# Batch 0's v on GpSimd's DMA queue ahead of w_in, q's halves from two queues, no f32 weight columns, j 8 later

## The chip, the cores and the metric

The kernel runs on one core of one Trainium2 chip. The metric is the device time of one execution in microseconds (us), given as the median of several executions. A profile shows one execution. Its span, from the first to the last instruction, is about 1.8 us shorter than the device time of the same execution (287.6 against 289.42 us for the kernel before).

## The reference

Eight batches of linear attention feed a two-layer block with a sine activation. Shapes: q, k, v are 8 x 8 heads x 576 tokens x 64; w_in is 512 x 2048, w_out 2048 x 512, alpha 2048; all f32.

```
q_s = softmax(q, over the 64 features)       # without 1/sqrt(d)
k_s = softmax(k, over the 576 tokens)
kv  = einsum('bhsd,bhse->bhde', k_s, v)
x   = einsum('bhsd,bhde->bhse', q_s, kv)      -> 4608 tokens x 512
h   = x @ w_in
g   = h + sin(alpha * h)**2 / (alpha + 1e-9)
out = g @ w_out
```

## The kernel before

The 4608 tokens are handled in nine tiles of 512. A tile takes 64 matmuls for h and 64 for the output, so TensorE is the engine to keep busy. One batch has 576 tokens, cut into nine slices of 64 ("j 0 to 8"; slice j holds the tokens 9p + j). Tile 0 needs only batch 0 (512 of its tokens, j 0 to 7), and tile 1 needs the other 64 tokens of batch 0 (j 8) and 448 of batch 1. Each engine works through its instructions in the order written below.

The start, as far as the change touches it:

```python
nc.scalar.dma_start(out=alpha_rows, in_=moe_alpha...)       # 8 KB, ScalarE's queue
load("q", q, 0, halves=True)                                # two transfers, sync queue
load("k", k, 0, halves=True)                                # two transfers, sync queue
for ii, j0, j1 in ((0, 0, 9), (1, 0, 5), (1, 5, 9)):
    nc.sync.dma_start(out=st[:, ii::2, j0:j1]..., in_=src_view(v, 0)...)
for x in range(2):                                          # w_in columns 0:256, as f32
    nc.sync.dma_start(out=wf[64 * x:64 * x + 64], in_=win_v[x][:, :, 0:256])
# ... identity, zeros ...
nc.tensor.transpose(tpa, alpha_rows, ident[0:nN, 0:nN])
DVE_CP(alpha_sb, tpa)                    # VectorE, ahead of everything on q
nc.vector.reciprocal(inva_sb, alpha_sb)
exp_q(0); exp_k(0)                       # ScalarE, one activation for each half
warm_up(7)
norm_q(0, [V, V])                        # VectorE: reduce, reciprocal, multiply; twice
GP_CP(held, staged["k", 0][:, 0, 0, 0:1])                   # GpSimd waits for k
for c0, c1 in ((256, 512), (512, 1024), (1024, 1536)):
    load_win(c0, c1)                     # GpSimd's queue, cast to bf16 in flight
GP_CP(win[:, :, 0:256], wf)              # the f32 columns, cast on GpSimd
load_win(1536, 2048); load_wout(0); load_wout(1)
# ... transposes of q, casts of v, two kv products, kv_norm -> kbd,
#     four attention products, copied to xT by ScalarE and VectorE in turn;
#     then the matmuls of h for tile 0 ...
```

Between tile 0 and tile 1 the 64 output matmuls of tile 0 are dealt out one by one (`take`) among the attention of batch 1:

```python
take(os, 10); [j 8 products of batch 0]; ACT_CP(xT[...], xp); take(os, 36)
exp_q(1); load("v", v, 1, halves=True); load_batch(2)
norm_q(1, ...); exp_k(1); q_transpose(1, ...); cast_v(1, [ACT_CP, DVE_CP])
take(os, 8)
kv_mm(1, 0); kv_norm(1, 0, 1); take(os, 2)
kv_mm(1, 1); kv_norm(1, 1, 2); take(os, 1)
# two pairs of attention products, each followed by take(os, 2); then take(os): the last 3
# then h of tile 1
```

The softmax here doesn't subtract the row's maximum and nothing guards it: scores larger than these inputs give would overflow.

## Time and profile before

The kernel took 289.31 us (median of 4, 289.01 to 289.61). These moments from the timeline:

| moment | us from the start |
|---|---|
| q's halves land / alpha lands | 4.50 and 5.98 / 2.83 |
| VectorE's first reduce of q starts | 5.72 |
| v's three pieces land | 10.96, 11.85, 12.97 |
| second kbd done / f32 columns of w_in cast | 14.92 / 16.17 |
| first h matmul of tile 0 | 16.23 |
| first output matmul of tile 0 | 30.05 |
| v of batch 1 lands (two halves) | 41.33, 42.71 |
| first h matmul of tile 1 | 47.76 |

### The profile page before, as it was taken

The numbers are of one execution on the slowest core, as the hardware profiler recorded it, in microseconds if no ns is written. First come the engines' busy times: TensorE is split into PE (matmuls) and PEld (weight loads), VectorE is DVE, ScalarE is ACT, GpSimd is POOL, SyncE is SP. The second block draws the span as 40 slices with busy tenths as digits, with TensorE's granted clock in tenths as the row PEclk, the third lists the DMA queues.
The fourth block names the chain that finished last, engine by engine and source line by source line (L and its number), as shares of the span: only waits on it lengthen the run. The fifth ranks groups of instructions, "written<-read, shape, count | busy, mean of one in ns | idle before, by whom it ended". The sixth has DMA issues, their size and how long they took to land.

```text
span 287.6 us, 4234 instructions
## 1 busy us (share of the span) xinstructions
PE 273.7 (95%) x1542; PEld 130.8 (45%) x1570; DVE 188.6 (66%) x280; ACT 227.2 (79%) x321; POOL 79.8 (28%) x73
## 2 busy tenths in 40 slices
PE   2889999999999999999999999999999999999994
PEld 1434454445454445444544454445444444444443
DVE  3867595889958667856776677757674555555412
ACT  5799775999479999899889988998877777777500
POOL 0679420675775571005300440032000000000000
PEclk9999999999999999999999999999999999999998
DMA  7999999935899957129910990116011111111142
GB/s 257 341 205 245 267 401 407 309 150 161 196 153 404 392 187 128 38 43 368 275 32 22 331 333 8 38 39 136 19 39 36 36 36 39 36 38 36 46 103 73
DMA packets 37893, 46.03 MB, mean 160 GB/s; under 512 B 15968, under 2 KB 21360, under 8 KB 37872
## 3 DMA queue, kind: packets, MB, share of 16 engines
q1 hardware_dynamic: 33392, 41.69, 47.5%
q0 software_dynamic: 4288, 3.93, 8.4%
q8 instruction: 12, 0.20, 0.3%
q10 hardware_dynamic: 192, 0.14, 0.2%
q14 instruction: 9, 0.07, 0.1%
HBM read 36.71 MB, written 9.44 MB: 160 GB/s over the span
## 4 chain that ended last, share of the span: by engine, by line
PE 83%; DMA 5%; POOL 4%; DVE 3%; issue 2%; SPq 1%; ACT 1%; POOLq 0%
PE hp L234 36%; PE op L254 34%; PE hp L254 4%; DMA st_w<-in_moe_w_in_dram 3%; POOL s L244 3%; PE kvp L157 2%; PE xp L206 2%; PE hh L234 1%; DMA qT<-qn 1%; PE op L538 1%; PE op L234 1%; ACT s L240 1%; DVE g L250 1%; DVE qs L144 1%; SPq L94 1%
## 5 line engine op out<-in xcount | busy, mean ns | idle before, releaser
L250 DVE SCALAR_TENSOR_TENSOR g<-s,inva_sb,hp 128x512 bf16<-128x512 f32 x130 | 96.2, 746 | 64.2 <-ACT s L242 54.2
L234 PE MATMUL hp<-xT,win 128*128 128x512 bf16 x512 | 129.2, 379 | 1.2 <-POOL win L320 0.6
L254 PE MATMUL op<-wout,g 128*128 128x512 bf16 x479 | 121.9, 379 | 1.1 <-issue 0.5
L240 ACT ACTIVATE s<-hp,alpha_sb 128x512 f32<-128x512 f32 x130 | 87.7, 682 | 25.8 <-PE hp L234 25.0
L234 PEld LDWEIGHTS <-win 128*128 128x128 bf16 x576 | 56.1, 98 | 68.3 <-POOL win L320 1.1
L254 PEld LDWEIGHTS <-g 128*128 128x128 bf16 x560 | 54.1, 98 | 61.7 <-issue 0.8
L242 ACT ACTIVATE s<-s 128x512 f32<-128x512 f32 x112 | 70.5, 630 | 3.5
L146 POOL TENSOR_TENSOR qn<-qe,qs 128x1152 bf16<-128x1152 bf16 x12 | 25.3, 2126 | 74.3 <-DVE qs L140 63.1
L244 POOL TENSOR_TENSOR s<-s 128x512 f32<-128x512 f32 x29 | 30.5, 1062 | 22.2 <-ACT s L240 21.6
L260 DVE COPY o<-op 128x512 f32<-128x512 f32 (+2 forms) x33 | 22.1, 670 | 9.7 <-PE op L254 5.8
L117 ACT ACTIVATE ke<-st_k 128x1152 bf16<-128x1152 f32 x16 | 17.9, 1151 | 3.0 <-DMA st_k<-in_k_dram 3.0
L117 ACT ACTIVATE qe<-st_q 128x1152 bf16<-128x1152 f32 x16 | 17.8, 1155 | 2.4 <-DMA st_q<-in_q_dram 2.3
L139 DVE TENSOR_REDUCE qs<-qe 128x36 f32<-128x2304 bf16 x5 | 12.8, 2553 | 8.7 <-ACT qe L117 8.6
L131 POOL CAST vb<-st_v 128x1152 bf16<-128x1152 f32 x12 | 13.6, 1162 | 10.1 <-DMA st_v<-in_v_dram 10.1
L254 PE MATMUL hp<-wout,g 128*128 128x512 bf16 x62 | 14.8, 379 | 0.2 <-issue 0.2
L209 DVE CAST xT<-xp 128x512 bf16<-128x512 f32 (+1 forms) x18 | 13.4, 743 | 0.0
L144 DVE TENSOR_REDUCE qs<-qe 128x18 f32<-128x1152 bf16 x6 | 8.0, 1330 | 4.6 <-ACT qe L117 4.6
L157 PE MATMUL kvp<-vb,ke 64*128 64x130 bf16 x288 | 9.9, 217 | 0.3 <-ACT vb L310 0.3
L117 ACT ACT_TABLE_LOAD x7 | 9.0, 1283 | 1.3 <-PEq L552 1.2
L157 PEld LDWEIGHTS <-ke 64*128 64x128 bf16 x288 | 8.2, 93 | 3.9 <-ACT s L242 1.3
L234 PE MATMUL hh<-xT,win 128*128 128x512 bf16 x39 | 9.4, 379 | 0.1
L206 PE MATMUL xp<-qT,kbd 128*128 128x256 bf16 (+1 forms) x40 | 8.2, 286 | 0.4 <-DVE xT L209 0.3
(68 smaller groups left out, 117.3 us busy)
## 6 DMA issues: line engine op xcount, KB each, us to landing
out_dram<-o SPq DMA_DIRECT2D x70, 128.0 KB, 2.4
st_q<-in_q_dram SPq DMA_DIRECT2D x6, 1152.0 KB, 6.6
st_k<-in_k_dram SPq DMA_DIRECT2D x6, 1152.0 KB, 8.5
st_v<-in_v_dram SPq DMA_DIRECT2D x6, 1152.0 KB, 10.3
st_q<-in_q_dram SPq DMA_DIRECT2D x4, 576.0 KB, 5.1
st_k<-in_k_dram SPq DMA_DIRECT2D x4, 576.0 KB, 7.1
wout<-in_moe_w_out_dram POOLq DMA_DIRECT2D x4, 512.0 KB, 9.6
st_v<-in_v_dram SPq DMA_DIRECT2D x3, 576.0 KB, 9.2
```

Source lines behind the costliest of these rows:

```text
L117: nc.scalar.activation(dst[:, :, ii * 128:(ii + 1) * 128].rearrange("p j (x d) -> p x j d", x=2), src[:, ii::2], AX.Exp)
L131: engs[ii](vv[:, 2 * ii:2 * ii + 2, :, 0:D], staged["v", b][:, ii::2])
L146: engs[ii % len(engs)].tensor_tensor(qn[:, ii].rearrange("p j (x d) -> p j x d", x=2), qe[:, ii], part.unsqueeze(3).to_broadcast([128, J, ...
L157: nc.tensor.matmul(kvp[:, e, ii * 130:(ii + 1) * 130], ke[r, j, ii * 128:(ii + 1) * 128], vt[r, j, ii * 130:(ii + 1) * 130], start=(j == 0 ...
L206: nc.tensor.matmul(xp[:, e, 0:n], kt[:, e, ii], qT[:, ii, j0:j1, e * 64:(e + 1) * 64], start=True, stop=True)
L234: nc.tensor.matmul(hp, win[:, ki, ni * 128:(ni + 1) * 128], xT[:, ki, t * MF:(t + 1) * MF], start=(ki == 0), stop=(ki == 3))
L240: nc.scalar.activation(s, hp, AX.Sin, scale=alpha_sb[:, ni:ni + 1])
L242: nc.scalar.activation(s, s, AX.Square)
L244: nc.gpsimd.tensor_tensor(s, s, s, op=ALU.mult)
L250: nc.vector.scalar_tensor_tensor(G[t][:, ni], in0=s, scalar=inva_sb[:, ni:ni + 1], in1=hp, op0=ALU.mult, op1=ALU.add)
L254: nc.tensor.matmul(acc, G[t][:, ni, j * 128:(j + 1) * 128], wout[:, ni, :], start=(ni == 0), stop=(ni == nN - 1))
L260: eng(o[:, cols], acc)
```

## The change

The intent is to feed the first h matmul sooner. GpSimd's f32 cast of the first 256 columns of w_in, which ended the wait for that matmul, goes away; v is requested on GpSimd's queue, followed at once by all of w_in; q's two halves are requested at the same moment from two queues; and the j 8 products move behind ten more output matmuls, with their copy on VectorE.

```diff
+    for ii, eng in ((0, nc.sync), (1, nc.scalar)):
+        eng.dma_start(out=st...[:, ii::2], in_=src_view(q, 0)[:, ii::2])
     nc.scalar.dma_start(out=alpha_rows, in_=moe_alpha...)
-    load("q", q, 0, halves=True)
     load("k", k, 0, halves=True)
-    [v in three pieces on nc.sync]
-    [w_in columns 0:256 as f32 on nc.sync]
 ...
+    GP_CP(held, staged["q", 0][:, 0, 0, 0:1])          # GpSimd waits for q's first half
+    [v in the same three pieces on nc.gpsimd]
+    for c0, c1 in ((0, 256), (256, 512), (512, 1024), (1024, 1536), (1536, 2048)):
+        load_win(c0, c1)
+    load_wout(0); load_wout(1)
 ...
-    [held on k; load_win of 256 to 1536; GP_CP(win[:, :, 0:256], wf); load_win(1536, 2048); w_out]
 ...
-        take(os, 10)
+        take(os, 20)
         [j 8 products]
-        ACT_CP(xT[:, :, 8 * P:9 * P], xp)
-        take(os, 36)
+        DVE_CP(xT[:, :, 8 * P:9 * P], xp)
+        take(os, 26)
```

More of the change, by code (lines that the diff above doesn't have):

```diff
@@ L268 @@
     V, GP = nc.vector, nc.gpsimd
+    staged["q", 0] = st = stage.tile([128, 4, J, D], F32, name="st_q", tag="st")
+    for ii, eng in ((0, nc.sync), (1, nc.scalar)):
+        eng.dma_start(out=st.rearrange("p i j d -> p i (j d)")[:, ii::2], in_=src_view(q, 0)[:, ii::2])
     nc.scalar.dma_start(out=alpha_rows, in_=moe_alpha.rearrange("(no ni) -> no ni", ni=128))
-    load("q", q, 0, halves=True)
     load("k", k, 0, halves=True)
-    staged["v", 0] = st = stage.tile([128, 4, J, D], F32, name="st_v", tag="st")
-    VJ = ((0, 0, 9), (1, 0, 5), (1, 5, 9))
-    for ii, j0, j1 in VJ:
-        nc.sync.dma_start(out=st[:, ii::2, j0:j1].rearrange("p i j d -> p i (j d)"),
-                          in_=src_view(v, 0)[:, ii::2, j0 * D:j1 * D])
-    wf = stage.tile([128, 4, J, D], F32, name="st_w", tag="st")[:, :, 0:4].rearrange("p c a b -> p c (a b)")
-    for x in range(2):
-        nc.sync.dma_start(out=wf[64 * x:64 * x + 64], in_=win_v[x][:, :, 0:256])
     make_identity(nc, ident)
@@ L298 @@
     nc.vector.reciprocal(inva_sb, alpha_sb)
+    GP_CP(singles.tile([128, 1], F32, name="held"), staged["q", 0][:, 0, 0, 0:1])
+    staged["v", 0] = st = stage.tile([128, 4, J, D], F32, name="st_v", tag="st")
+    for ii, j0, j1 in ((0, 0, 9), (1, 0, 5), (1, 5, 9)):
+        GP.dma_start(out=st[:, ii::2, j0:j1].rearrange("p i j d -> p i (j d)"),
+                     in_=src_view(v, 0)[:, ii::2, j0 * D:j1 * D])
+    for c0, c1 in ((0, 256), (256, 512), (512, 1024), (1024, 1536), (1536, 2048)):
+        load_win(c0, c1)
+    for c in range(2):
+        load_wout(c)
     exp_q(0)
@@ L315 @@
     q_tile(0)
-    GP_CP(singles.tile([128, 1], F32, name="held"), staged["k", 0][:, 0, 0, 0:1])
-    for c0, c1 in ((256, 512), (512, 1024), (1024, 1536)):
-        load_win(c0, c1)
-    GP_CP(win[:, :, 0:256], wf)
-    load_win(1536, 2048)
-    for c in range(2):
-        load_wout(c)
     q_transpose_ii(0, 0, 0, 8, tps[0])
```

## The prediction

> **What bounds the kernel now.** I read the table of cores first: one core, 287.6 us, granted clock 0.997, so nothing is throttled. Then the page: TensorE is busy 95% of the span, and its idle time is nearly all in the first slices. The table of stretches says how much: in 16.2 to 30 us the matmuls fill 13.66 of 13.80 us, and in 100 to 140 us 39.63 of 40.
>
> ```profile
> PE 273.7 (95%) x1542; PEld 130.8 (45%) x1570; DVE 188.6 (66%) x280; ACT 227.2 (79%) x321; POOL 79.8 (28%) x73
> 0.00:16.20 16.20, 8.86 (x72) 4.33 (x72) 10.94 (x24) 10.54 (x13) 6.48 (x15) 1.00 0.97 288
> 16.20:30.00 13.80, 13.66 (x62) 6.27 (x65) 9.55 (x16) 13.05 (x21) 12.08 (x14) 1.00 1.21 242
> 30.00:33.00 3.00, 2.72 (x17) 1.19 (x15) 2.58 (x6) 1.29 (x3) 2.29 (x3) 1.00 1.21 231
> ```
>
> After the stretch and its length come the busy times of TensorE, weight loads, VectorE, ScalarE and GpSimd, then clock, DMA share and GB/s. A busy TensorE need not be at its rate, so I checked the rate: in the chain of waits 16 matmuls of h take 3.45 us, 0.2157 each. The 64 of the first token tile at that rate are 13.80 us; the first starts at 16.23 and the output matmuls start at 30.05, which is 13.82 later. So from 16.23 on TensorE has work without a hole, and **the change can save what it brings that start forward, plus holes of a few tenths later**.
>
> What holds the start? In the timeline of the first microseconds (start, length, what, and in brackets the idle time before it and what ended it):
>
> ```profile
> 4.53 1.16 ACT L117 ACTIVATE qe<-st_q 128x1152 bf16<-128x1152 f32 x1 [2.02 <-DMA st_q<-in_q_dram]
> 5.72 1.35 DVE L144 TENSOR_REDUCE qs<-qe 128x18 f32<-128x1152 bf16 x1 [2.00 <-ACT qe L117]
> 10.37 1.36 DVE L146 TENSOR_TENSOR qn<-qe,qs 128x1152 bf16<-128x1152 bf16 x1
> 13.00 0.63 ACT L310 CAST vb<-st_v 128x512 bf16<-128x512 f32 x1 [0.81 <-DMA st_v<-in_v_dram]
> 14.33 0.59 DVE L170 TENSOR_TENSOR kbd<-kvp,kvr 64x128 bf16<-64x128 f32 x2
> 14.96 1.36 DVE L342 CAST xT<-hp 128x512 bf16<-128x512 f32 x2
> 15.13 1.04 POOL L320 CAST win<-st_w 128x1024 bf16<-128x1024 f32 x1 [2.32 <-DMA st_w<-in_moe_w_in_dram]
> 16.23 1.90 PE L234 MATMUL hp<-xT,win 128*128 128x512 bf16 x7 [0.65 <-POOL win L320]
> ```
>
> Two paths end together. The weights: the f32 columns land at 15.00 and GpSimd's cast ends at 16.17. The attention: the first xT piece is done at 15.34 (half of ScalarE's pair from 14.69), the last at 16.32 (VectorE's pair from 14.96). The chain names the weights, 9.68 us of DMA. With the weights free, the first matmul could go at 15.34, but the sixth (row ni=0, ki=3) would still wait for 16.32.
>
> **What the Trainium skill says.** *DMA: Bandwidth & Descriptors*, "Issuing engines are not separate DMA queues": DMAs from sync, scalar and gpsimd share the same 16 engines, and several issuers save only issue time. The trace agrees: in 2 to 12 us the engines are full (281 to 407 GB/s), so a second issuer adds no bandwidth there.
>
> The same page, "Queues, rings and completion order", has each engine go round the rings packet by packet. The trace looks more like first come, first served. Batch 1's q is requested at 24.60 while w_out is under way, and for two microseconds only GpSimd's queue moves:
>
> ```profile
> DMA packets 414, 0.41 MB, mean 205 GB/s; under 512 B 13, under 2 KB 414, under 8 KB 414
> q0 software_dynamic: 414, 0.41, 123.6%
> ```
>
> That is 24.6 to 26.6 us. Likewise w_in, requested from 8.75, has 8 packets through by 13.0. So v, requested on GpSimd's queue while k is under way, should neither overtake k nor wait for long.
>
> *SBUF — State Buffer*, the box on the "DVE blocks DMA" trap: VectorE in a two-port mode locks GpSimd out of writing descriptors. Here, six w_in requests beside a busy VectorE took 0.62 to 0.84 us each; if the lock acts, it costs some 0.2 us. *TensorE: Matmul & The Clock Gate*, Part 1: the array runs at half clock until it has been busy some 3.4 us. The trace agrees: seven warm-up matmuls from 5.74 take 3.15 us (0.45 each), the six from 9.65 take 1.49 (0.25).
>
> **The change part by part.**
>
> *Weights.* Gone are two f32 transfers (0.5 MB), their two requests and the 1.04 us cast. The first 256 columns come cast in flight, right behind v. Single transfer records show v landing at 10.96, 11.85 and 12.97, but most engines are through with v near 11.5 and one or two lag by 1.5 us. The column packets took 60 ns each against 46 for the f32 ones, so 256 columns take about 1.5 us: from 11.5, with the laggards, they should land between 13.2 and 14.5. That is 1.7 to 3 us before 16.17. The weights leave the path. GpSimd has eight semaphores for its DMAs, so its ninth request waits for the first v; enough is queued by then.
>
> *q from two queues, alpha behind it.* Before, the q halves land at 4.50 and 5.98 and alpha at 2.83. Now both halves are requested at about 0.74 and share the engines. By sharing evenly, both land near 5.3 to 5.7 (the bytes are those that landed by 5.98, less a faster ramp: the first full half microsecond is 3.0 to 3.5). So the first exponential, due at 4.53, starts near 5.4. And alpha is now behind the second half in ScalarE's ring, so it lands near 5.5. This matters, because the order of instructions keeps alpha's copy and reciprocal on VectorE ahead of the first reduce: before, from landing (2.83) to the end of that reciprocal (3.72) was 0.9 us, so VectorE can't begin to reduce before about 6.4. Either way the reduce moves from 5.72 to about 6.6: a delay **d of 0.9 us**. If the rings are served in turn by whole requests, q's first half lands as before and alpha alone sets d, 0.3 to 0.7.
>
> *What d does.* From 5.72 to 12.6 VectorE has no gap, and TensorE's transposes and first kv product hang on it, so the first kbd ends at 13.98 + d. The second product was bound by v's last piece (0.26 us of wait), so some of d vanishes. With d = 0.9: kbd ends at 14.88, reciprocal 0.18 and second kbd 0.59 with short gaps end at 15.72, two xT copies of 0.68 on VectorE end at 17.12. The sixth matmul of h starts there, and 59 x 0.2157 = 12.73 follow: 29.85 against 30.05, a gain of 0.2. By the same sum d = 0.3 (last copy 16.52) gains 0.8, d = 0 gains 1.0, d = 1.5 loses 0.4. Break-even is d = 1.1.
>
> *j 8 later.* Ten more output matmuls go ahead of the small attention products. Before, those waited for a buffer:
>
> ```profile
> 32.74 0.28 PE L214 MATMUL xp<-qT,kbd 128*128 128x64 bf16 x4 [0.28 <-DVE g L250]
> 33.06 0.37 ACT L396 CAST xT<-xp 128x256 bf16<-128x256 f32 x1 [1.74 <-PE xp L214]
> 33.45 1.28 ACT L117 ACT_TABLE_LOAD   x1
> ```
>
> Ten matmuls (2.16 us) cover the wait until the buffer comes free: a gain of 0.28. The copy moves to VectorE, which idles 2.59 us before its next reduce; ScalarE can load the exponential's table up to 1.7 us sooner. But batch 1's k and v are set by DMA (38.28 and 41.35), and TensorE has output matmuls in that time, so this is hidden.
>
> *Transfers sooner.* The first 25 us move the same source bytes, without the slack around 12 to 14 us where the rate was half. Weights, w_out and batch 1 should land about 1 us earlier. From 33 to 48 us TensorE idles only 0.21 more, mostly in normalisation steps that no DMA sets; from 70 to 100 us it idles 0.86. I put 0.15 on all of this.
>
> **The rivals.** (1) *The intended result*: neither split nor alpha costs anything and v's tail comes sooner; start gain 1.0, sum 1.4, 288.1 us. For it: the weights are what the chain names. Against: alpha's place in the ring. (2) *A new wait takes over*: q's first half and alpha late, so VectorE's chain replaces the weights; start gain 0.2, sum 0.6, 288.9. I think this the likeliest. (3) *v late or in k's way*: GpSimd is held until q's first half lands, then a 0.71 us copy and three requests of 0.6 to 0.8, the last near 8.4 if q lands at 5.4; k is done at 9.47, so there is some margin, but if the rings shared fairly, k would land later, exponentials of k and ScalarE's copies behind it would slide by 1 us or more, and the start would be 0.5 us later than before: 289.8. Against it: the first-come behaviour above. (4) *The transfer hidden anyway*: TensorE bound by ScalarE or VectorE just after the start, so that an earlier start buys only waiting. Against: in 16.2 to 30 us TensorE, not they, has no holes; it would make 289.3.
>
> **Range and chances.** Start: 0.55 x 0.2 + 0.3 x 0.8 - 0.15 x 0.4 = 0.29. With 0.28 for the buffer wait and 0.15 for the transfers: 0.72 us, from 289.55 to 288.8. The three runs of before spread over 0.6 us. The rivals span 288.1 to 289.8; with the spread I take 287.8 to 289.7. A change of 2% is 5.8 us; TensorE's whole idle time after 16.2 us is under 7 us, more than half of it at the very end, so faster by 2% gets 0.01, and slower, which would need a stalled queue, 0.01.
>
> **What would show it.** Right: no GpSimd cast of w_in; the first h matmul waits for xT, not for a DMA; first h between 15.3 and 16.2, first output matmul at 29.1 to 30.0; alpha lands after 5 us; the first reduce starts at 6.2 to 6.9; no VectorE wait before the j 8 products. Wrong in size: the first reduce still near 5.7 (then rival 1), or k's landing beyond 9.8 (rival 3). Wrong in kind: a wait of h for w_in columns, or holes in TensorE between 17 and 30 us.

## The result

The changed kernel took 289.62 us (median of 4, 289.56 to 289.95), where the kernel before took 289.31. The ratio is 1.0013 with a 95% interval of 0.9996 to 1.0030: the same. The 0.7 us that were expected did not come.

First the page of the changed kernel (its line on busy times), then its table of stretches, with the columns as in the prediction:

```profile
PE 275.4 (96%) x1570; PEld 130.8 (45%) x1570; DVE 188.6 (66%) x281; ACT 226.5 (79%) x320; POOL 81.7 (28%) x77
0.00:16.20 16.20, 8.18 (x70) 4.08 (x70) 9.41 (x22) 9.43 (x11) 10.24 (x21) 1.00 0.96 265
16.20:30.00 13.80, 13.65 (x63) 6.14 (x64) 10.19 (x18) 13.22 (x22) 9.47 (x11) 1.00 1.21 233
30.00:33.00 3.00, 2.98 (x14) 1.27 (x13) 2.48 (x6) 2.92 (x4) 2.92 (x3) 1.00 1.18 266
```

TensorE's total rose by 1.7 us although it does the same work: 1570 matmul records were kept against 1542. So this line can't be compared to a microsecond. The stretch of 30 to 33 us can: TensorE has no hole there now.

The timeline of the changed kernel shows the start. The columns are as in the prediction: start, length, engine and line, what, and in brackets the idle time before it.

```profile
5.80 2.22 ACT L117 ACTIVATE qe<-st_q 128x1152 bf16<-128x1152 f32 x2 [2.71 <-DMA st_q<-in_q_dram]
6.58 0.25 PE L289 MATMUL warm<-ident,alpha_rows 16*128 16x16 f32 x1 [6.58 <-DMA alpha_rows<-in_moe_alpha_dram]
6.87 0.17 DVE L290 COPY alpha_sb<-warm 128x16 f32<-128x16 f32 x1 [4.43 <-PE warm L289]
7.25 1.29 DVE L144 TENSOR_REDUCE qs<-qe 128x18 f32<-128x1152 bf16 x1
15.70 0.59 DVE L170 TENSOR_TENSOR kbd<-kvp,kvr 64x128 bf16<-64x128 f32 x2
16.35 0.60 PE L214 MATMUL hp<-qT,kbd 128*128 128x512 bf16 x2 [0.24 <-DVE kbd L170]
16.79 1.52 PE L234 MATMUL hp<-xT,win 128*128 128x512 bf16 x6
```

VectorE stands idle for 4.43 us and then does alpha before it does q, because that is the order of its instructions. Its first reduce starts at 7.25 instead of 5.72, and everything behind it slides: the second kbd ends at 16.29 instead of 14.92, and the first h matmul is at 16.79, 0.56 us later than before. The weights are no longer what it waits for: the first columns land at 13.08 and 13.73.

The chain of waits (start, length, what) of the changed kernel names the same two things in its first 50 us:

```profile
1.27 5.18 DMA alpha_rows<-in_moe_alpha_dram
...
33.27 10.52 DMA st_v<-in_v_dram
```

The second line is v of **batch 1**. It lands at 42.35 and 43.79, 1.0 and 1.1 us later than before, and tile 1's h starts at 48.26, 0.50 us later. The experiments need both lines.

### The profile page after: what moved, and what is told of

It reads as the page before. It is cut to its first block, busy times and chain, and to the rows that moved or that the text cites. A ratio compares the mean times of both kernels' runs of the same rounds, so it can differ in the third digit from the quotient of the medians.

```text
span 287.8 us, 4258 instructions
## 1 busy us (share of the span) xinstructions
PE 275.4 (96%) x1570; PEld 130.8 (45%) x1570; DVE 188.6 (66%) x281; ACT 226.5 (79%) x320; POOL 81.7 (28%) x77
## 4 chain that ended last, share of the span: by engine, by line
PE 76%; DMA 7%; DVE 6%; ACT 4%; POOL 3%; issue 2%; ACTq 0%; SPq 0%; POOLq 0%
PE hp L234 34%; PE op L254 33%; DMA st_v<-in_v_dram 4%; POOL s L244 3%; ACT s L240 3%; PE kvp L157 2%; DMA alpha_rows<-in_moe_alpha_dram 2%; DVE qs L144 2%; PE xp L206 2%; DMA qT<-qn 1%; PE op L534 1%; PE op L234 1%; PE hh L234 1%; DVE qn L146 1%; DVE o L260 1%
## 5 line engine op out<-in xcount | busy, mean ns | idle before, releaser
L254 PE MATMUL op<-wout,g 128*128 128x512 bf16 x496 | 124.2, 379 | 0.0
L131 POOL CAST vb<-st_v 128x1152 bf16<-128x1152 f32 x12 | 13.6, 1164 | 10.1 <-DMA st_v<-in_v_dram 10.1
```

What stands on the lines that cost most here:

```text
L254: nc.tensor.matmul(acc, G[t][:, ni, j * 128:(j + 1) * 128], wout[:, ni, :], start=(ni == 0), stop=(ni == nN - 1))
```

## The experiments

Each run was timed in 5 or 6 executions against the kernel before on the same chip. Runs e1 to e4 shared one chip and the kernel before's runs (median 289.37), e5 to e8 another (289.26), e9 to e11 a third (289.89); e12 was timed by itself later (289.50).

The theory after the result: *alpha, queued behind q's second half, delays VectorE, and so eats what the freed weights gained*. Its rivals: q's halves side by side are what delays; or v on GpSimd's queue does.

### e1: the changed kernel again

No edit.

> The changed kernel once more, unaltered, as the yardstick of this chip and for the noise. Theory (q's sharing and alpha's place delay VectorE's first reduce, and what the freed weights gain is lost to it): first exponential of q at about 5.8 us, alpha landing at about 6.4, first reduce at 7.25, first h matmul at 16.8, first output matmul at 30.7; ratio to before 1.000 to 1.002. Rival (the 0.3 us are noise of chips or states): the ratio changes sign, below 0.999.

Measured: 289.64 us, ratio 1.0005 (0.9990 to 1.0019). Alpha landed at 6.32, the first reduce started at 7.12 and the first output matmul at 30.54. The result holds in a second session.

### e2: alpha first

```diff
+    nc.scalar.dma_start(out=alpha_rows, ...)
     [q halves on nc.sync and nc.scalar]
-    nc.scalar.dma_start(out=alpha_rows, ...)
```

> The changed kernel with alpha requested ahead of q's second half on ScalarE's queue; q's halves still come from two queues. Theory: alpha lands before 4 us and VectorE no longer waits for it; q's first half still shares the engines and lands at 5.2 to 5.8, so the first reduce starts at 6.4 to 7.0 instead of 7.25 to 7.3, the first output matmul is 0.3 to 0.9 us earlier than in the changed kernel, and the time is 0.3 to 0.9 us lower. Rival (alpha's place costs nothing, the delay is all q's sharing): the first reduce stays at 7.2 or later and the time does not move. Rival (v on GpSimd's queue is the cause): no change either.

Measured: 288.70 us, ratio 0.9976 (0.9962 to 0.9989), and 0.94 us below e1 of the same rounds. The edit moves one 8 KB request. It also puts q's second half 0.49 us behind the first, so two delays end at once; e4 takes them apart. The timeline of this run:

```profile
5.86 1.35 DVE L144 TENSOR_REDUCE qs<-qe 128x18 f32<-128x1152 bf16 x1 [2.14 <-ACT qe L117]
```

The reduce now waits for q's exponential alone, and starts 1.26 us before that of e1. I had expected 6.4 to 7.0, because q's first half was to share the engines with the second. It did not: requested 0.49 us ahead of the second half, it landed at 4.64, and the second half at 7.05. The head start put the halves in a row. The DMA totals from 3 to 4 us show it, first of the changed kernel, then of e2 (q1 is the sync queue, q10 ScalarE's; packets, MB, busy share of the engines):

```profile
q1 hardware_dynamic: 98, 0.23, 57.0%
q10 hardware_dynamic: 77, 0.18, 45.1%
```

```profile
q1 hardware_dynamic: 175, 0.40, 101.7%
q10 hardware_dynamic: 1, 0.00, 0.6%
```

### e3: q on one queue, alpha alone

```diff
-    [q halves on nc.sync and nc.scalar]
     nc.scalar.dma_start(out=alpha_rows, ...)
+    load("q", q, 0, halves=True)
```

> The changed kernel with q's halves one after the other on the sync queue and alpha alone on ScalarE's queue, as before the change; v, w_in and j 8 as changed. Theory: q's first half lands at 4.5, alpha at 2.8, first reduce at 5.7; the second kbd ends at 14.7 to 15.0, first h at 15.3 to 15.5, first output matmul at 29.2 to 29.4 (0.7 to 0.9 us before the kernel before), and with 0.3 us from j 8 the time is 0.9 to 1.2 us below before, ratio 0.996 to 0.997. Rival (v through GpSimd's queue is late or in k's way): k lands after 9.8 or v after 13.3, first h at 16 or later, ratio about 1.000.

Measured: 288.98 us, ratio 0.9987 (0.9971 to 1.0002). The start did what the theory said, within 0.25 us: reduce at 5.94, second kbd done at 15.04, first h at 15.54, first output matmul at 29.41, which is 0.64 us before that of the kernel before. The time fell short of the 0.9 to 1.2 us expected. Rival 3 of the prediction is out: k landed at 9.33 and v at 13.09. The difference from e2 (0.28 us) is within the spread of their runs, so splitting q gave nothing measurable here.

### e4: alpha late, q on one queue

```diff
-    [q halves on nc.sync and nc.scalar]
-    nc.scalar.dma_start(out=alpha_rows, ...)
+    load("q", q, 0, halves=True)
+    nc.sync.dma_start(out=alpha_rows, ...)
```

> As the run with q on one queue, but alpha is requested on the sync queue behind both q halves and ahead of k: alpha is late without q's halves sharing the engines. Theory: q's first half lands at 4.5 and its exponential ends at 5.7, but alpha lands at about 6.0, so the first reduce starts only at 6.7 to 6.9: a delay of 1.0 to 1.2 us from alpha alone; the first output matmul is at 30.0 to 30.3, ratio 0.999 to 1.000. Rival (alpha harmless): first reduce at 5.7 and the time of the run with q on one queue.

Measured: 289.86 us, ratio 1.0013 (0.9998 to 1.0027). Against e3 of the same rounds, which differs in alpha's place only, the time is 0.88 us longer and the first output matmul is at 30.35 instead of 29.41. (First reduce, first output matmul and ratio all lie a little above the ranges expected.) The timeline of e4:

```profile
6.56 0.17 DVE L288 COPY alpha_sb<-warm 128x16 f32<-128x16 f32 x1 [4.13 <-PE warm L287]
6.77 0.25 DVE L289 RECIPROCAL inva_sb<-alpha_sb 128x16 f32<-128x16 f32 x1
6.94 1.29 DVE L144 TENSOR_REDUCE qs<-qe 128x18 f32<-128x1152 bf16 x1
```

q's first half landed at 4.60 and its exponential was done at 5.78, yet the reduce waited until 6.94, for alpha. So **a late alpha alone costs about 0.9 us**, without any sharing between q's halves. (k, behind alpha on the same queue, also landed 0.55 us later than in e3, but nothing waited for it: VectorE works without a gap from 6.56 to 13.6, and TensorE's first kv product starts at 13.60 straight after its transposes.) In the changed kernel both delays happen at once, and q's own exponential (5.80 + 1.16 = 6.96) would have held the reduce nearly as long as alpha did. So the first rival isn't out: sharing alone would have cost some 1.2 us of the 1.5 by this estimate, and no run has the halves side by side with an early alpha.

### Where the rest of the start gain goes: e5, e6, e7

In e2 and e3 the output matmuls of tile 0 start 0.6 to 0.7 us earlier than before, but h of tile 1 starts at 47.85 and 47.65, where it was 47.76. The timeline of e2 shows the loss:

```profile
42.00 1.17 ACT L131 CAST vb<-st_v 128x1152 bf16<-128x1152 f32 x1 [0.26 <-DMA st_v<-in_v_dram]
43.22 0.69 PE L157 MATMUL kvp<-vb,ke 64*128 64x130 bf16 x18 [0.80 <-ACT vb L131]
43.41 0.76 DVE L131 CAST vb<-st_v 128x1152 bf16<-128x1152 f32 x1 [1.76 <-DMA st_v<-in_v_dram]
```

TensorE idles 0.80 us ahead of batch 1's kv product, for the cast in the first line, which waits for v of batch 1; the third line is the same for the second product. The DMA engines are saturated all that time (a share of 1.04 to 1.21 in every stretch from 16.2 to 48 us; it passes 1 because the records overlap), so in this order of requests v can't come sooner. The theory then: **bandwidth up to batch 1's v is a second bound**, just behind the first. To test it I took 1 MB of traffic away ahead of that v, with wrong results on purpose:

```diff
-        late = {..., 10: lambda: load_wout(3), 13: ...}
+        late = {..., 13: ...}
-        nc.tensor.matmul(acc, G[t][...], wout[:, ni, :], ...)
+        nc.tensor.matmul(acc, G[t][...], wout[:, ni % 12, :], ...)
```

The last matmuls of the kernel, which index w_out by columns, got the same edit. It was applied to the kernel before (e5), the changed one (e6) and alpha first (e7).

> Wrong result on purpose: the kernel before without the load of the last quarter of w_out (1 MB of f32 source; the matmuls read an earlier quarter in its place, so TensorE's work is the same). It takes 2.5 us of transfers away ahead of batch 1's v and tells whether the second token tile waits for bandwidth. Theory (transfers are saturated from 3 us to past 43 us, and batch 1's v is the last thing the second tile waits for): v's halves land near 38.8 and 40.2 instead of 41.3 and 42.7, but in the kernel before TensorE only gets to batch 1's kv product at 43.5, so h of tile 1 starts at 47.4 to 47.8 and the time falls by 0 to 0.3 us. Rival (what limits is ScalarE's and VectorE's chain in batch 1, not the landing): the same shift in this and in the two companion runs.

> Wrong result on purpose: the changed kernel without the load of the last quarter of w_out. Theory: v of batch 1 lands near 41 instead of 43.8; TensorE arrived at the kv product about when v did, so it gains 0.2 to 0.6 us against the changed kernel (h of tile 1 at 47.6 to 48.0). Rival: no gain, or as much as in the kernel before.

> Wrong result on purpose: the run with alpha first, without the load of the last quarter of w_out. Theory: there TensorE stood 1.17 us between matmuls ahead of batch 1's kv product, waiting for v; with v landing near 40.8 that hole closes, h of tile 1 starts at 46.6 to 47.0 instead of 47.85, and the time falls 0.8 to 1.2 us below the run with alpha first, ratio to before 0.993 to 0.995: the gain at the start then comes through to the end. Rival (the start gain is lost on ScalarE or VectorE): the hole stays and the ratio stays near 0.9975.

| | median us | ratio (95%) | v of batch 1 lands | first output matmul | h of tile 1 |
|---|---|---|---|---|---|
| e5, before | 288.71 | 0.9979 (0.9945 to 1.0012) | 38.60, 40.04 | 30.08 (was 30.05) | 47.38 (was 47.76) |
| e6, changed | 289.10 | 0.9979 (0.9950 to 1.0008) | 39.40, 40.79 | 30.51 (was 30.66) | 47.65 (was 48.26) |
| e7, alpha first | 287.86 | 0.9935 (0.9908 to 0.9961) | 38.74, 40.17 | 29.39 (was 29.32) | 46.52 (was 47.85) |

The stage from first output matmul to h of tile 1 shortened by 0.41 us in e5, 0.46 in e6 and 1.40 in e7. That is the order that the theory gave, and not the equal shift of the rival. (These are readings of one profile each; the ratios of e5 and e6 alone don't exclude 1, that of e7 does. The edit also takes a 0.80 us request from GpSimd, but from 16.5 to 50 us TensorE waits in e2 only for the cast and 0.2 us for kbd, never for GpSimd.) In e7 the wait is gone from the timeline:

```profile
42.26 0.68 PE L157 MATMUL kvp<-vb,ke 64*128 64x130 bf16 x18
```

e5 gained a little more than expected, and not through v. Without the load GpSimd has one request (0.80 us) less among its squares, so the buffer for the j 8 products came free sooner: they started at 32.36 instead of 32.74, and the whole 0.38 us was gained there.

### e8 and e11: only the j 8 part, twice

The edit is the last part of the change's diff on the kernel before.

> The kernel before with only the j 8 part of the change. Theory: the 0.28 us wait of TensorE at 32.7 us goes away; TensorE reaches batch 1's kv product 0.28 us sooner, and since v's second half has to land at 42.7 and be cast by VectorE until 43.5, at most 0.3 us are gained: h of tile 1 at 47.4 to 47.7, ratio 0.9990 to 1.0000. Rival (the copy on VectorE delays batch 1's reduce and so the transposes): h of tile 1 later than 47.8.

> The kernel before with only the j 8 part once more, because the profile of its first run began 2 us late. Expectation unchanged: no wait ahead of the j 8 products, h of tile 1 at 47.4 to 47.7, ratio 0.9990 to 1.0000.

Measured: 289.16 us, ratio 0.9996 (0.9960 to 1.0031), and 289.81 us, ratio 0.9990 (0.9955 to 1.0025). The wait ahead of the j 8 products is gone in both profiles, but any gain in time lies within the noise, so the 0.3 us is neither shown nor refuted. Both profiles fell on executions with a slow start, the second one too, so the expected 47.4 to 47.7 for h of tile 1 could not be read off. In both, v's last piece landed at 13.85 instead of 12.97 and the f32 columns at 15.82 and 15.95 instead of 15.00. The timeline of e11:

```profile
17.18 1.90 PE L234 MATMUL hp<-xT,win 128*128 128x512 bf16 x8 [0.72 <-POOL win L320]
```

In e8 something else came on top. The granted clock was 0.52 from 17.0 to 20.5 us, and h's matmuls start 0.43 us apart from 18.26 to 20.39 instead of 0.22. Its first output matmul is at 32.56, 15.51 us after its first h matmul, where the kernel before needs 13.82. So about 1.7 us of that execution's delay goes with the clock, and not with the transfers.

The kernel before has such executions as well. Its times on the chips of e5 to e12 range from 288.78 to 291.72. Kernels with v and w_in on GpSimd's queue spread less there: e7 spans 287.74 to 288.06, e10 288.38 to 289.20, e6 289.00 to 289.36. (e9, below, doesn't: 290.52 to 293.20, with long pauses of TensorE of its own.) So ratios to the kernel before from these sessions hold its bad executions too, and look better than a comparison of medians. Why the sync queue's tail is late in some executions I did not find out.

### e10: alpha first, without the j 8 part

The edit: e2 with the `take` counts and the copy as before the change.

> The run with alpha first, with the j 8 part taken back. Theory: TensorE gets a wait of about 0.3 us again ahead of the j 8 products near 32 us, but the hole ahead of batch 1's kv product (1.17 us there, set by v's landing) shrinks by as much, so h of tile 1 stays at 47.7 to 48.0 and the time within 0.15 us of the run with alpha first: j 8 is worth nothing where v's landing bounds. Rival (j 8 is worth its 0.28 us everywhere): 0.3 us slower than the run with alpha first.

Measured: 288.85 us, ratio 0.9964 (0.9933 to 0.9995). The wait ahead of the j 8 products is back (a gap of 0.66 us between matmul starts at 32.01, where an unbroken stream has 0.22), and h of tile 1 started at 47.97 against 47.85. The time is 0.15 us above e2's, on another chip. So j 8 later is worth next to nothing where batch 1's v sets the next stage, as expected.

### e9: a candidate that failed

The last quarter of w_out is requested behind batch 1's v, and TensorE does batch 1's kv products ahead of the last 16 output matmuls.

```diff
-        late = {..., 10: lambda: load_wout(3), 13: ...}
+        late = {..., 13: ...}
         load("v", v, 1, halves=True)
+        load_wout(3)
 ...
-        take(os, 8); kv_mm(1, 0); kv_norm(1, 0, 1); take(os, 2); kv_mm(1, 1); ...   # 8 taken in between
+        take(os, 2); kv_mm(1, 0); kv_norm(1, 0, 1); kv_mm(1, 1); kv_norm(1, 1, 2); ...; take(os)
```

> A candidate that should beat both: the run with alpha first, and the last quarter of w_out is requested behind batch 1's v instead of ahead of it; on TensorE batch 1's kv products go ahead of the last 16 output matmuls. Theory (bandwidth ahead of batch 1's v sets the second tile): v of batch 1 lands at about 40.2 instead of 43.4, w_out's last quarter at 42.7 to 43.5, the 16 output matmuls (3.45 us) follow, and h of tile 1 starts at 47.0 to 47.5 instead of 47.85: 0.3 to 0.8 us below the run with alpha first, ratio 0.995 to 0.9967. Rival (the wait only moves to w_out's last quarter, because TensorE has nothing to fill it with): h of tile 1 at 47.8 or later, no gain.

Measured: 291.33 us, ratio 1.0056 (1.0019 to 1.0093): slower than the kernel before, and its fastest execution (290.52) is above every one of the changed kernel (289.24 to 289.95). The rival was right, and more. v's second half landed at 42.62, not 40.2, since w_out's quarter, requested 0.2 us behind it, landed at 42.33 beside it. And with nothing to fill in, TensorE stood still twice. The waits of TensorE from 16.5 to 50 us in e9 (who waited for whom: us in total, times, longest):

```profile
PE kvp L157 <- ACT vb L131: 1.0, 1, 1.0
PE kvp L157 <- DVE vb L131: 0.9, 1, 0.9
```

After those pauses its matmuls ran at half rate for a while: their starts are 0.43 us apart at 46.67, and 0.22 from 47.0 on. The table of stretches has the granted clock at 0.50 there (third number from the right):

```profile
43.50:46.90 3.40, 3.36 (x24) 1.57 (x25) 1.75 (x6) 0.91 (x1) 0.00 (x0) 0.50 1.04 406
```

h of tile 1 started at 50.03.

### e12: a version that beats both

e2 with one number changed: three of the output matmuls that followed the last attention product go ahead of batch 1's first kv product, into the hole.

```diff
-        take(os, 8)
+        take(os, 11)
         kv_mm(1, 0, ps_e, split=True)
```

> A second candidate that should beat both kernels: the run with alpha first, with 11 instead of 8 output matmuls of tile 0 ahead of batch 1's first kv product and so 3 fewer behind the last attention product. Theory (TensorE stands about 0.8 us before that product because batch 1's v has not landed, and has 5 output matmuls left at the end): the hole shrinks by 3 x 0.2157 = 0.65 us, h of tile 1 starts at 47.1 to 47.4 instead of 47.85, its third slice of xT is ready by 48.1, and the time falls 0.3 to 0.65 us below the run with alpha first, ratio to before 0.9945 to 0.9965. Rival (those matmuls were covering the copies of xT, so the wait moves behind them): h of tile 1 starts early but its matmuls stand still until 48 and more, and the time stays within 0.2 us of the run with alpha first.

Measured: **288.02 us** (287.87 to 288.26), ratio 0.9939 (0.9913 to 0.9965), with correct results. The median is 0.68 us below e2's, a little more than expected, but e12 and e2 were not timed in the same rounds. The ratios (0.9939 and 0.9976) make it look like 1.1 us, because the kernel before had slower executions in e12's session (up to 290.98, against 290.02). The timeline of e12:

```profile
42.94 0.68 PE L157 MATMUL kvp<-vb,ke 64*128 64x130 bf16 x18
...
46.56 3.66 PE L234 MATMUL hp<-xT,win 128*128 128x512 bf16 x16
```

The hole is filled, and h of tile 1 starts at 46.56 and runs through without a gap, so those three matmuls had not been needed behind the product. 0.65 us of the 1.29 us against e2's profile are the three matmuls. The rest fits v landing sooner in this execution (42.72 against 43.39). Only two small moves separate e12 from the changed kernel: alpha's request, and three matmuls.

## Why the prediction was right or wrong

The time lay in the range, 289.62 in 287.8 to 289.7, near its upper end, and "within 2%" was right. The forecast gain of 0.7 us was not: the measured difference is 0.3 us the other way and not clear of noise. That the range held it was its width, drawn around rivals from 288.1 to 289.8, and some luck; three of the signs that it named for being right failed: the first h matmul at 16.79 (15.3 to 16.2), the first output matmul at 30.66 (29.1 to 30.0), the first reduce at 7.25 (6.2 to 6.9). By its own steps:

- **What bounds.** Right up to the first output matmul; what sets tile 1 was missed (last point). The start of h was the place, and the weights left the path as worked out (landing 13.08 and 13.73, where 13.2 to 14.5 was estimated). Rival 3 did not occur: v landed at 12.57, k at 9.04. (A small misreading: from 2 to 4 us the DMA engines were not full before the change, their share was 0.86.)
- **d, the delay of VectorE's first reduce.** This is the step that failed. The mechanism was named, alpha behind q in ScalarE's ring and ahead of q on VectorE, but the term was sized at 0.9 us and measured 1.5 (7.25 against 5.72). Alpha landed at 6.44, not at 5.5, and q's first half at 5.77, where 5.3 to 5.7 was estimated. The prediction's own break-even was d = 1.1. For d = 1.5 its sum gives a loss of 0.4 at the first output matmul; 0.61 was measured. What the sum left out: the last attention product (16.57 to 16.79) stands ahead of h in TensorE's order, so the stream of h can't start before it ends. The same 0.2 us is missing elsewhere: in e2 and e3 d was 0.14 and 0.22, for which it gives a gain of about 0.9, and 0.73 and 0.64 were measured at the first output matmul. By that measure nothing would have been left of the gain of 0.2 at the likeliest d, 0.9.
- **The weight of that chance.** d = 1.5 got 0.15, d = 0.3 got 0.3. Of the expected start gain of 0.29 us, 0.24 came from the case d = 0.3, which did not happen. For a small d, two delays (alpha's and that of q's sharing) had to be small together, and I gave that case too much.
- **j 8.** The wait of 0.28 us did go away (the attention products follow their predecessors without a gap at 35.16), but neither e8, e11 nor e10 shows it in the time.
- **Transfers sooner.** Wrong in sign. They came later: v of batch 1 by 1.0 to 1.1 us, and in e2, where the start was earlier than in the kernel before, still by 0.65 to 0.68 us. Part of that lies in the prediction's reading. The halved rate at 12 to 14 us (233 GB/s) was in good part not slack: the DMA share there was 1.25, and 202 to 207 GB/s at a share of 1.24 or more stood until 24 us, while weights were cast in flight and counted in bf16 bytes. Nor do the same source bytes take the same time: the first 256 columns are 512 records, of 60 ns each when cast in flight and of 46 ns as f32. By an estimate from these, spread over 16 engines, that is 1.9 us in place of 1.5, where the prediction had 1.5 for the cast ones. In 14.5 to 16 us the changed kernel moved less than before; these are the DMA totals of that stretch, first of the kernel before, then of the changed one:

```profile
DMA packets 351, 0.30 MB, mean 203 GB/s; under 512 B 22, under 2 KB 351, under 8 KB 351
```

```profile
DMA packets 237, 0.20 MB, mean 130 GB/s; under 512 B 17, under 2 KB 237, under 8 KB 237
```

  I did not take apart what slowed the engines there; GpSimd was issuing its requests one by one behind landings then (its w_out request waited 0.85 us for a landing at 16.16), and e2, with the same queue order and an earlier start, moved 0.29 MB in the same stretch.
- **What was missing altogether.** That batch 1's v sets tile 1. The prediction saw that k and v of batch 1 "are set by DMA" and used it to call a ScalarE gain hidden, but counted the start gain in full. e2, e3 and e7 show that the start gain is hidden in the same way unless the transfers or TensorE's order give way: e7 gained 1.40 us in that stage from 1 MB less traffic.

Of the changed kernel's delays, 0.61 us stood at the first output matmul, 0.50 at h of tile 1, 0.32 at the first sine of tile 2 (79.77 against 79.45) and 0.33 at that of the last tile (250.53 against 250.20), in line with the 0.31 us between the medians. The 0.2 us that came back in tile 1 I did not trace.

## What to carry to other kernels

A small transfer that something early in an engine's order depends on must be requested ahead of large ones on its queue, or its consumer must stand later in that engine's order: 8 KB behind q's two halves of 576 KB cost 0.9 us here (e4 against e3). Before counting a gain at the start, look for the next wait that the same time runs into; here it was bandwidth up to the second tile's v. Work moved into that hole came close to what taking the transfer away gave (e12 288.02 us, e7 287.86, on different chips), but an order with nothing to fill the hole lost more than the hole (e9, 291.33).

## What the Trainium skill lacked or had wrong

- *DMA: Bandwidth & Descriptors*, "Queues, rings and completion order", has each engine go round its rings packet by packet. It does not say that a head start decides: q's halves requested at the same moment from two queues landed at 5.77 and 6.23, but with 0.49 us between the requests at 4.64 and 7.05. With both requested together the queues did take turns (0.23 and 0.18 MB from 3 to 4 us); with the head start one moved 0.40 MB and the other none. That what is already queued goes first is my reading of this; the traces don't show why.
- *DMA: Bandwidth & Descriptors*, "Issuing engines are not separate DMA queues", says that several issuers only save issue time. They can also cost: two issuers put the halves side by side, and the first half, which the chain needed, came at 5.77 instead of 4.50.
- *TensorE: Matmul & The Clock Gate*, Part 1, agreed: after two pauses of 1.0 and 0.9 us close together in e9, matmul starts were 0.43 us apart, then 0.22. Its rule of thumb of idle gaps over about 3 us (under "Why this matters for your kernels") was too mild here: neither gap was half that long. Small attention matmuls lay between them. The granted clock was 0.50 from 43.5 to 46.9 us. In e8 it fell to 0.52 after waits of 0.83, 0.36 and 0.59 us; in e11, after 1.07, 0.36 and 0.72, it did not. So a pause of that length can be enough, but need not be.
- *DMA: Bandwidth & Descriptors*, "SWDGE vs HWDGE vs iDMA", gives a packet from GpSimd's queue as at most 4096 bytes by preference. It does not say that the same v load moves in larger records from there than from the sync queue: those of v's first half are of 4608 bytes, 178 ns each, against 2304 bytes, 93 ns each. The rate per engine is about the same (25.9 and 24.8 bytes per ns).
